# The low half of a folded weight in an attention and feed-forward kernel: subtracted on VectorE before, on TensorE after

## The chip, the cores and the metric

The kernel runs on one core of one Trainium2 chip. The metric is the device time of one execution in microseconds (us), as the median of several runs.

## The reference, cut to what matters

Attention with a local window of 96 keys and 8 global keys (4 batches, 8 heads, 768 positions, 64 numbers a head) gives 3072 tokens of 512 numbers each. On these goes a feed-forward part without a nonlinear function but with a product of two branches:

```
a = x @ w1                    # x: 3072 x 512, w1 and w2: 512 x 1024
b = x @ w2
h = a * b @ w3                # w3: 1024 x 1024
return h @ w_out              # w_out: 1024 x 512
```

Since nothing stands between w3 and w_out, the kernel multiplies these two once, at the start (the fold), and uses the 1024 x 512 product in place of both.

## The kernel before, in words

All of the large products run on TensorE in a rounded format (fp32r, one pass). To keep the accuracy of fp32, each operand is split in a high part (the value rounded to fp32r) and a low part (value minus high part), and three products are summed: high by high, high by low, low by high. This holds for w1 and w2 (tiles `w12h`, `w12l`), for the attention's output (`xh`, `xl`), for a*b (`gh`, `gl`) and for the folded weight (`wh`, and `wl`, eight blocks of 128 x 512).

The fold itself runs in fp32: for each of the eight blocks f, eight products `F.f.k` (L190) are summed over k in one PSUM bank (`prod[f]`, w_ in the rows). Each of these 64 products appears as two matmuls in the trace. Ahead of that VectorE makes the weights from 64-bit input words, three instructions (L168, L170, L172) a piece. When a block is whole, three steps follow, in the order of the names in `ORDER`: `pe.f` (ScalarE copies the bank to SBUF, tile `raw`, L195), `ph.f` (ScalarE rounds `raw` to `wh`, L198), `pl.f` (VectorE subtracts, `wl` = `raw` - `wh`, L203).

The first part of the program is written out by hand as a long string of names, `ORDER`, and runs in that order on every engine. Other names in it are: `S.s`, the scores of step s (TensorE, L577, from `qr` into the tiles `sc` and `more`); `R`, `E`, `s`, `c`, `X`, the softmax of a step (row maxima on VectorE; exponentials L593 on ScalarE; reciprocal of the sums on VectorE; scaling L608 on ScalarE; transposition L619 on VectorE, into `pt`); `V.d`, the values of two steps (TensorE, L633, from `pt` into `sc`); `h.d` and `l.d`, the split of their result (`xh` L656 on ScalarE, `xl` L661 on VectorE); `wh.f` and `wl.f`, the split of a block of w1 and w2 (L179 on ScalarE, L183 on VectorE); `U.f.n.i`, the first feed-forward products (L223 to L225), and `a`, `g`, `gh`, `gl`, the steps behind them; `Z`, the second feed-forward products (L251 to L253). The fold's banks, `more` and the banks of U and Z come from one pool of four PSUM banks, `ps_m`, and a bank is given out again when its last reader is done.

Behind `ORDER` come the other batches in a loop, with the same products and without any fold.

Of the kernel before, what the change touches and what calls it, by code (L numbers as in the profile page):

```python
# [10 lines left out]
F32 = mybir.dt.float32  # L11
F32R = mybir.dt.float32r
BF16 = mybir.dt.bfloat16
I32 = mybir.dt.int32
AF = mybir.ActivationFunctionType
ALU = mybir.AluOpType
PSUM = bass.MemoryType.PSUM

B, H, S, D = 4, 8, 768, 64
DM, DF, DO = 512, 1024, 512  # L20
P = 128
# [6 lines left out]
NFC = DF // P  # L28
WIN = 96
GLB = 8  # L30
R = 32
# [18 lines left out]
FIRST = 5  # L50
# [1 line left out]
nt bias d.h0 d.o0 d.h1 d.o1 A.h0 B.h0 C.h0 d.k1 A.o0 B.o0 d.o2 A.h1 C.o0 F.0.0 d.k2 B.h1 F.1.0 A.o1 d.k3 C.h1 B.o1 F.2.0 A.k1 d.o3 C.o1 F.3.0 B.k1  # L52
A.o2 d.K2 C.k1 A.k2 F.0.1 B.o2 B.k2 F.1.1 C.o2 F.2.1 C.k2 bD biasA d.O2 F.3.1 A.k3 A.o3 B.k3 F.0.2 B.o3 F.1.2 C.k3 d.q0 A.K2 F.2.2 C.o3 F.3.2 d.K3
B.K2 F.0.3 A.O2 F.1.3 C.K2 F.2.3 d.O3 B.O2 S.0 C.O2 F.3.3 d.q1 R.0.0 F.0.4 R.0.1 E.0.0 R.0.2 F.0.5 E.0.1 R.0.3 d.T5 E.0.2 A.K3 F.1.4 E.0.3 B.K3 F.1.5
F.2.4 A.O3 d.W0 B.O3 F.2.5 F.3.4 s.0 C.O3 c.0 F.3.5 S.1 C.K3 d.T4 A.T5 F.0.6 B.T5 F.0.7 d.v0 X.0 F.1.6 pe.0 ph.0 F.2.6 d.T6 R.1.0 R.1.1 E.1.0 F.1.7
C.T5 E.1.1 F.2.7 R.1.2 pe.1 F.3.6 d.q2 R.1.3 E.1.2 F.3.7 pl.0 E.1.3 A.T4 F.5.0 d.T7 pe.3 A.W0 F.5.1 ph.3 s.1 B.T4 c.1 F.5.2 B.W0 F.5.3 d.q3 F.5.4 A.T6
ph.1 F.5.5 X.1 pe.2 ph.2 F.5.6 pl.1 V.0 B.T6 pl.2 C.T6 F.5.7 h.0 C.W0 d.W4 F.6.0 pe.5 l.0 ph.5 F.6.1 wh.0 pl.5 S.2 S.3 d.W3 wl.0 F.6.2 pl.3 R.2.0
F.6.3 R.2.1 E.2.0 F.6.4 R.2.2 E.2.1 R.2.3 F.6.5 C.T4 E.2.2 F.6.6 E.2.3 A.T7 d.W1 s.2 B.T7 c.2 F.6.7 C.T7 d.q5 F.4.0 pe.6 F.4.1 X.2 ph.6 d.v1 F.7.0
R.3.0 F.7.1 R.3.1 E.3.0 R.3.2 F.7.2 d.q4 E.3.1 R.3.3 F.7.3 A.W1 E.3.2 F.7.4 B.W1 E.3.3 F.7.5 s.3 pl.6 F.7.6 c.3 C.W1 F.4.2 F.4.3 wh.1 F.4.4 X.3 F.4.5
wl.1 V.1 A.W3 B.W3 C.W3 F.7.7 h.1 d.W2 F.4.6 wh.3 l.1 F.4.7 pe.7 wl.3 ph.7 S.4 S.5 pe.4 pl.7 ph.4 U.0.0.0 R.4.0 R.4.1 E.4.0 pl.4 U.0.0.1 E.4.1 A.W2  # L60
B.W2 U.0.1.0 a.0 C.W2 U.0.1.1 R.4.2 wh.2 d.W6 R.4.3 U.1.0.0 E.4.2 wl.2 E.4.3 U.1.0.1 g.0 s.4 gh.0 U.1.1.0 A.W4 c.4 gl.0 B.W4 U.1.1.1 C.W4 U.2.0.0 a.1
X.4 wh.4 d.W5 U.2.0.1 g.1 U.2.1.0 a.2 wl.4 gh.1 U.2.1.1 gl.1 A.W6 B.W6 U.3.0.0 C.W6 U.3.0.1 A.W5 wh.6 d.W7 U.3.1.0 B.W5 a.3 U.3.1.1 wl.6 d.v2 C.W5
U.4.0.0 g.2 wh.5 U.4.0.1 g.3 gh.2 wl.5 U.4.1.0 gh.3 a.4 gl.2 U.4.1.1 gl.3 A.W7 B.W7 C.W7 U.5.0.0 d.q7 g.4 wh.7 R.5.0 U.5.0.1 gh.4 R.5.1 d.q6 R.5.2
# [17 lines left out]
class FeedForward:  # L81
# [3 lines left out]
    def __init__(self, ctx, tc, w12, w3k, w3t, w_out, out):  # L85
        self.nc = tc.nc
        self.w12, self.w3k, self.w3t, self.w_out, self.out = w12, w3k, w3t, w_out, out
        self.wp = wp = ctx.enter_context(tc.tile_pool(name="wp", bufs=1))
        self.mp = ctx.enter_context(tc.tile_pool(name="mp", bufs=2))
        self.ps = ctx.enter_context(tc.tile_pool(name="ps_m", bufs=4, space=PSUM))  # L90
        self.w = [wp.tile([P, NFC, 2, NCC, P], F32R, name=f"w12{x}") for x in "hl"]
        self.wh, self.wl = wp.tile([P, NFC, DO], F32R, name="wh"), [None] * NFC
        self.places, self.free, self.raw = list(range(NFC)), [NFC], {}

        self.wo = self.mp.tile([P, NFC, DO], I32, tag="gh", bufs=1, name="wo")
        gl = self.mp.tile([P, 2, 4 * PC], I32, tag="gl", bufs=1, name="stage")
        self.slots = [gl[:, i] for i in range(2)]
        self.t3, self.kt, self.prod, self.got = {}, {}, {}, {}
# [90 lines left out]
        block = self.kt[k // 2][:, (k % 2 * NFH + f) * P:][:, :P] if f < NFH else self.t3[f][:, k * P:(k + 1) * P]  # L189
        self.nc.tensor.matmul(self.prod[f], lhsT=block.bitcast(F32), rhs=self.wo[:, k].bitcast(F32), start=k == 0, stop=k == NFC - 1)  # L190

    def fold_out(self, f):
        i = self.places.pop(0)
        self.raw[f] = i, self.wp.tile([P, DO], F32, tag=f"wl{i}", name=f"raw_{f}")
        self.nc.scalar.activation(self.raw[f][1], self.prod[f], AF.Copy)  # L195

    def fold_high(self, f):
        self.nc.scalar.activation(self.wh[:, f], self.raw[f][1], AF.Copy)  # L198

    def fold_low(self, f):  # L200
        i, raw = self.raw[f]
        self.wl[f] = self.wp.tile([P, DO], F32R, tag=f"wl{self.free.pop()}", name=f"wl_{f}")
        self.nc.vector.tensor_tensor(out=self.wl[f], in0=raw, in1=self.wh[:, f].bitcast(F32), op=ALU.subtract)  # L203
        self.free.append(i)


class Unit:
# [227 lines left out]
def strided(ap, *dims):  # L435

    return bass.AP(ap.tensor, ap.offset, [ap.ap[0], *dims])
# [15 lines left out]
def banded(ctx, tc, ff, ns, nt, n1, nf, oki, qk, vx, sc, pr):  # L453


    nc = tc.nc

    xp = ctx.enter_context(tc.tile_pool(name="xp", bufs=2))
    bp = ctx.enter_context(tc.tile_pool(name="bp", bufs=1))
# [10 lines left out]
    def warm(i):  # L470

        if not warmth:
            x = at.tile([P, P], BF16, tag="pt", name="warm")
            nc.vector.memset(x, 0.0)
            warmth.extend((x, ff.ps.tile([P, 96], F32, tag="m", name="warmed")))
        x, y = warmth
        for _ in range(WARM[i]):
            nc.tensor.matmul(y, lhsT=x[:, :P], rhs=x[:, :96], start=True, stop=True)
# [3 lines left out]
    def distances():  # L482

        n = KF + NR * GLB
        it = bp.tile([P, n], I32, name="it")
        gi = bp.tile([P, NR * GLB], I32, name="gi")
        sl = bp.tile([P, 2], F32, name="sl")
        dist, out = (bp.tile([P, n], F32, name=x) for x in ("dist", "out"))
        gd = bp.tile([P, NR * GLB], F32, name="gd")
        win, glob, own = slice(0, P), slice(P, KF), slice(KF, n)  # L490
        for hp in range(NP):
            x = it[hp * R:(hp + 1) * R]
            nc.gpsimd.iota(x[:, win], pattern=[[-1, P]], base=WIN, channel_multiplier=1)
            nc.gpsimd.iota(x[:, glob], pattern=[[1, GLB]], base=0, channel_multiplier=1)
            nc.gpsimd.iota(x[:, own].rearrange("p (q g) -> p q g", g=GLB), pattern=[[R, NR], [-1, GLB]], base=0, channel_multiplier=1)
        nc.gpsimd.iota(gi.rearrange("p (q g) -> p q g", g=GLB), pattern=[[0, NR], [1, GLB]], base=0, channel_multiplier=0)
        for h in range(H):
            hp, u = divmod(h, 2)
            nc.gpsimd.memset(sl[hp * R:(hp + 1) * R, u:u + 1], -SLOPES[h] / SCALE)
        nc.vector.tensor_copy(out=n1, in_=nt)  # L500
        nb = ff.ps.tile([P, 4], F32, tag="m", name="nb")
        nc.tensor.matmul(nb, lhsT=one, rhs=n1, start=True, stop=True)
        warm(1)
        nc.vector.tensor_copy(out=dist, in_=it)
        nc.vector.tensor_scalar(out=out, in0=dist, scalar1=0.0, scalar2=None, op0=ALU.is_lt)
        nc.scalar.activation(nf, nb, AF.Copy)
        nc.gpsimd.tensor_scalar(out=gd, in0=gi, scalar1=ng, scalar2=FAR, op0=ALU.is_ge, op1=ALU.mult)
        nc.gpsimd.tensor_scalar(out=gd, in0=gd, scalar1=nl, scalar2=None, op0=ALU.max)
        flat = pr.rearrange("p q u w -> p (q u w)").rearrange("p (n k) -> p n k", k=PW * 2 // 3)
        nc.scalar.activation(flat, strided(warmth[0], [0, NR * 3], [1, PW * 2 // 3]), AF.Copy)  # L510
        late.extend((sl, dist, out, gd, own))
# [38 lines left out]
    def frame(s, q):  # L550

        return (0 if s % NB else WIN - R * q), KF
# [48 lines left out]
    def scale(s, engine):  # L601
        sm = stats[s][1]
        if engine is nc.scalar:
            for q in range(NR):
                w0, w1 = frame(s, q)
                for u in range(2):
                    x = pr[:, q, u, GLB + w0:GLB + w1]
                    nc.scalar.activation(x, x, AF.Copy, scale=sm[:, q, u:u + 1])  # L608
        else:
            x = pr[:, :, :, GLB:GLB + KF]  # L610
            nc.vector.tensor_tensor(out=x, in0=x, in1=strided(sm, [2, NR], [1, 2], [0, KF]), op=ALU.mult)
# [64 lines left out]
        warm(0)  # L676

    units = {}
    do = dict(A=lambda *x: ff.convert(0, *x), B=lambda *x: ff.convert(1, *x), C=lambda *x: ff.convert(2, *x), wh=ff.high, wl=ff.low, F=ff.fold, pe=ff.fold_out, ph=ff.fold_high, pl=ff.fold_low, S=scores, R=maxima, E=exponentials, s=sums, c=lambda s: scale(s, nc.scalar if s < FIRST else nc.vector), X=turn, V=values, h=high, l=low, bias=distances, bD=masks, biasA=biases, nt=sizes)
    do.update((name, lambda *x, method=method: getattr(units[0], method)(*x)) for name, method in (("U", "first"), ("a", "gate"), ("g", "product"), ("gh", "high"), ("gl", "low"), ("Z", "second"), ("ot", "store")))  # L680

    def ordered():
# [88 lines left out]
```

## Time and profile before

| | |
|---|---|
| median of 3 runs | 524.25 us (523.61 to 524.45) |
| the profiled execution, its own time | 523.78 us |
| its span, first to last instruction | 521.9 us |
| granted TensorE clock, mean | 1.000 |
| TensorE matmul busy | 514.7 us, 99% of the span |
| TensorE weight loads busy | 404.0 us, 77% |
| VectorE busy | 263.7 us, 51% |
| ScalarE busy | 197.0 us, 38% |

The busy time of TensorE's matmuls counts overlapped instructions once; how fast it advances is read from the distance of the matmuls' starts. About two microseconds of the time lie outside the span. In the rows PE is TensorE, PEld its weight loads, DVE VectorE, ACT ScalarE, POOL GpSimd.

### The profile page before, as it was taken

The page shows a single profiled execution, that of the slowest core. Times are in us where ns is not written, and L with a number is a line of the kernel's source. Part 1 is how long each engine was busy: PE and PEld are TensorE (multiplying, and loading weights), DVE is VectorE, ACT ScalarE, POOL GpSimd, SP SyncE. Part 2 cuts the span into 40 slices and gives each one's busy share as a digit, 9 for nine tenths or more (in the row PEclk, how much of TensorE's full clock was granted, in tenths as well). Part 3 has the DMA queues.
Part 4 walks back from the last instruction along what each step waited for, and adds up shares of the span by engine and source line. Part 5 has one row for each costly group of instructions (what it writes and reads, how often), then busy time and mean ns, then how long its engine had stood idle before and what let it go on. Part 6 is the DMA issues. An engine that isn't in the chain of part 4 may idle for free. (4 is left out here: it accounts for less than half of the span.)

```text
span 521.9 us, 12884 instructions
## 1 busy us (share of the span) xinstructions
PE 514.7 (99%) x5572; PEld 404.0 (77%) x5572; DVE 263.7 (51%) x690; ACT 197.0 (38%) x600; POOL 4.3 (1%) x29
## 2 busy tenths in 40 slices
PE   8999999999999999999999999999999999999997
PEld 5345468888888888888888888888888888888885
DVE  7999999993627337028345046263155352022210
ACT  2557766453435244134243134243253351212210
POOL 2000000000000000000000000000000000000000
PEclk9999999999999999999999999999999999999999
DMA  8997833612350130240130240130240101100001
GB/s 311 370 394 275 344 104 103 267 40 82 120 184 36 36 124 3 63 180 1 62 116 20 76 147 0 48 115 30 93 135 0 64 1 41 43 0 0 1 26 60
DMA packets 13842, 53.71 MB, mean 103 GB/s; under 512 B 1363, under 2 KB 3411, under 8 KB 11731
## 3 DMA queue, kind: packets, MB, share of 16 engines
q1 hardware_dynamic: 13632, 52.57, 27.8%
q8 instruction: 45, 0.74, 0.6%
q10 hardware_dynamic: 146, 0.26, 0.1%
q14 instruction: 19, 0.15, 0.1%
HBM read 46.53 MB, written 6.29 MB: 101 GB/s over the span
## 5 line engine op out<-in xcount | busy, mean ns | idle before, releaser
L223 PE MATMUL m<-xh,w12h 128*128 128x512 f32 x384 | 150.9, 393 | 0.0
L224 PE MATMUL m<-xl,w12h 128*128 128x512 f32 x384 | 149.5, 389 | 0.0
L225 PE MATMUL m<-xh,w12l 128*128 128x512 f32 x384 | 149.4, 389 | 0.0
L223 PEld LDWEIGHTS m<-xh,w12h 128*128 128x128 f32 x384 | 72.1, 188 | 16.7 <-ACT pr L593 1.7
L593 ACT ACTIVATE pr<-pr,mx 128x136 f32<-128x136 f32 (+2 forms) x192 | 74.5, 390 | 26.4 <-DVE mx L586 26.1
L225 PEld LDWEIGHTS m<-xh,w12l 128*128 128x128 f32 x384 | 72.1, 188 | 15.1
L224 PEld LDWEIGHTS m<-xl,w12h 128*128 128x128 f32 x384 | 72.1, 188 | 14.4
L251 PE MATMUL o<-wh,gh 128*128 128x512 f32 x184 | 72.5, 394 | 0.0
L252 PE MATMUL o<-wl,gh 128*128 128x512 f32 x184 | 71.8, 390 | 0.0
L253 PE MATMUL o<-wh,gl 128*128 128x512 f32 x184 | 71.6, 389 | 0.0
L233 DVE TENSOR_TENSOR ag<-m,ag 128x512 f32<-128x512 f32 x48 | 32.8, 685 | 71.5 <-PE m L225 65.8
L238 ACT ACTIVATE gh<-ag 128x512 fp32r<-128x512 f32 x48 | 30.1, 629 | 95.6 <-DVE ag L233 95.6
L661 DVE TENSOR_TENSOR xl<-sc,xh 128x1024 fp32r<-128x1024 f32 x12 | 14.7, 1224 | 73.9 <-ACT xh L656 73.9
L230 ACT ACTIVATE ag<-m 128x512 f32<-128x512 f32 x48 | 28.4, 592 | 46.4 <-PE m L225 44.1
L265 ACT ACTIVATE ot<-o 128x512 f32<-128x512 f32 x23 | 13.8, 599 | 77.7 <-PE o L253 77.7
L243 DVE TENSOR_TENSOR gl<-ag,gh 128x512 fp32r<-128x512 f32 x48 | 32.7, 682 | 16.4 <-ACT gh L238 16.3
L253 PEld LDWEIGHTS o<-wh,gl 128*128 128x128 f32 x184 | 34.5, 188 | 7.6
L251 PEld LDWEIGHTS o<-wh,gh 128*128 128x128 f32 x184 | 34.5, 188 | 7.5 <-issue 0.2
L252 PEld LDWEIGHTS o<-wl,gh 128*128 128x128 f32 x184 | 34.5, 188 | 6.9
L619 DVE STREAM_TRANSPOSE pt<-pr 128x1280 f32<-128x1280 f32 x24 | 36.1, 1506 | 1.3 <-ACT pr L608 1.2
L593 ACT ACTIVATION_READ_ACCUMULATOR pr<-pr,mx 128x1 f32 x192 | 36.1, 188 | 0.0
L633 PEld LDWEIGHTS sc<-pt,vr 32*64 32x64 f32 x2112 | 30.5, 130 | 5.0 <-issue 4.3
(97 smaller groups left out, 421.0 us busy)
## 6 DMA issues: line engine op xcount, KB each, us to landing
qr<-qk SPq DMA_DIRECT2D x20, 720.0 KB, 6.4
vr<-vx SPq DMA_DIRECT2D x8, 768.0 KB, 4.4
out_dram<-ot SPq DMA_DIRECT2D x23, 256.0 KB, 2.0
raws<-w SPq DMA_DIRECT2D x5, 1024.0 KB, 4.9
stage<-w3t SPq DMA_DIRECT2D x3, 1024.0 KB, 7.7
vr<-vx SPq DMA_DIRECT2D x4, 576.0 KB, 3.8
qr<-qk SPq DMA_DIRECT2D x4, 528.0 KB, 7.5
more_raws<-w SPq DMA_DIRECT2D x2, 1024.0 KB
```

The source lines that it names most:

```text
L223: self.nc.tensor.matmul(ps, lhsT=mh, rhs=xh[:, i], start=i == 0, stop=False)
L224: self.nc.tensor.matmul(ps, lhsT=mh, rhs=xl[:, i], start=False, stop=False)
L225: self.nc.tensor.matmul(ps, lhsT=ml, rhs=xh[:, i], start=False, stop=i == NCC - 1)
L233: self.nc.vector.tensor_tensor(out=self.g[f], in0=self.ps[f, 1], in1=self.a[f], op=ALU.mult)
L238: self.nc.scalar.activation(self.gh[:, f], self.g[f], AF.Copy)
L243: self.nc.vector.tensor_tensor(out=self.gl[:, f], in0=self.g[f], in1=self.gh[:, f].bitcast(F32), op=ALU.subtract)
L251: self.nc.tensor.matmul(ps, lhsT=self.gh[:, f, ts], rhs=ff.wh[:, f], start=f == 0, stop=False)
L252: self.nc.tensor.matmul(ps, lhsT=self.gh[:, f, ts], rhs=ff.wl[f], start=False, stop=False)
L253: self.nc.tensor.matmul(ps, lhsT=self.gl[:, f, ts], rhs=ff.wh[:, f], start=False, stop=f == NFC - 1)
L593: nc.scalar.activation(x, x, AF.Exp, bias=mx[:, q, u:u + 1], scale=-1.0, accum_out=sm[:, q, u:u + 1])
L619: nc.vector.transpose(strided(pts[d][:, half * 2 * NR * PF:], [PF, 2 * NR], [P, NR + 1], [1, R]), x.rearrange("p n (k c) -> p n k c", c=R))
L633: nc.tensor.matmul(sc[cols, hp, n0 * R:n1 * R], lhsT=v[rows, i, cols], rhs=turned, start=i == i0, stop=i == NV - 1, skip_group_check=True)
```

## The change

The same two halves of a folded block are made in another way. ScalarE rounds the bank straight to `wh` (`pe.f` is now `fold_high`). TensorE then multiplies `wh` by minus the unit matrix and adds the result onto the same bank, so that the bank holds value minus high part (`ph.f` is now `fold_rest`). ScalarE copies the bank to `wl` (`pl.f` is now `fold_low`). The tiles `raw` go, VectorE's eight subtractions go, and the bank of a block is given back after the second copy instead of the first. Minus the unit matrix is made once, at the start, by two GpSimd instructions and one ScalarE copy. In `ORDER` the names `ph` and `pl` stand at other places.

```diff
-F.2.4 A.O3 d.W0 B.O3 F.2.5 F.3.4 s.0 C.O3 c.0 F.3.5 S.1 C.K3 d.T4 A.T5 F.0.6 B.T5 F.0.7 d.v0 X.0 F.1.6 pe.0 ph.0 F.2.6 d.T6 R.1.0 R.1.1 E.1.0 F.1.7
+F.2.4 A.O3 d.W0 B.O3 F.2.5 F.3.4 s.0 C.O3 c.0 F.3.5 S.1 C.K3 d.T4 A.T5 F.0.6 B.T5 F.0.7 d.v0 X.0 F.1.6 pe.0 F.2.6 d.T6 R.1.0 R.1.1 E.1.0 F.1.7 ph.0
...
-        self.places, self.free, self.raw = list(range(NFC)), [NFC], {}
+        self.minus = wp.tile([P, P], F32R, name="minus")
...
-    def fold_out(self, f):
-        i = self.places.pop(0)
-        self.raw[f] = i, self.wp.tile([P, DO], F32, tag=f"wl{i}", name=f"raw_{f}")
-        self.nc.scalar.activation(self.raw[f][1], self.prod[f], AF.Copy)
-
     def fold_high(self, f):
-        self.nc.scalar.activation(self.wh[:, f], self.raw[f][1], AF.Copy)
+        self.nc.scalar.activation(self.wh[:, f], self.prod[f], AF.Copy)
+
+    def fold_rest(self, f):
+
+        self.nc.tensor.matmul(self.prod[f], lhsT=self.minus, rhs=self.wh[:, f], start=False, stop=True, skip_group_check=True)
 
     def fold_low(self, f):
-        i, raw = self.raw[f]
-        self.wl[f] = self.wp.tile([P, DO], F32R, tag=f"wl{self.free.pop()}", name=f"wl_{f}")
-        self.nc.vector.tensor_tensor(out=self.wl[f], in0=raw, in1=self.wh[:, f].bitcast(F32), op=ALU.subtract)
-        self.free.append(i)
+        self.wl[f] = self.wp.tile([P, DO], F32R, tag=f"wl{f}", name=f"wl_{f}")
+        self.nc.scalar.activation(self.wl[f], self.prod[f], AF.Copy)
...
+        eye = bp.tile([P, P], F32, name="eye")
+        make_identity(nc, eye)
...
+        nc.scalar.activation(ff.minus, eye, AF.Copy, scale=-1.0)
```

The order of the instructions on each engine, read at three places. First TensorE and ScalarE around blocks 0 and 1, ahead of the values of the first two steps (`V.0`). A block's bank is a w_ with a number of its own: block 0 is w_221 before and w_228 after, block 1 is w_225 and w_232, block 3 is w_236 and w_243, block 5 is w_457 and w_465. TensorE before:

```order
L577 MATMUL sc<-qr_331 32x136 x32
L190 MATMUL w_221<-wo,kt_352 128x512 x2
L190 MATMUL w_225<-wo,kt_352 128x512
L190 MATMUL w_231<-wo,kt_352 128x512
L190 MATMUL w_225<-wo,kt_352 128x512
L190 MATMUL w_231<-wo,kt_352 128x512
L190 MATMUL w_236<-wo,kt_352 128x512 x2
L190 MATMUL w_457<-wo,t_5_411 128x512 x7
L633 MATMUL sc<-pt_418,vr_416 64x128 x8
```

and TensorE of the change:

```order
L577 MATMUL sc<-qr_338 32x136 x32
L190 MATMUL w_228<-wo,kt_359 128x512 x2
L190 MATMUL w_232<-wo,kt_359 128x512
L190 MATMUL w_238<-wo,kt_359 128x512
L190 MATMUL w_232<-wo,kt_359 128x512
L197 MATMUL w_228<-wh,minus 128x512
L190 MATMUL w_238<-wo,kt_359 128x512
L190 MATMUL w_243<-wo,kt_359 128x512 x2
L197 MATMUL w_232<-wh,minus 128x512
L190 MATMUL w_465<-wo,t_5_418 128x512 x3
L197 MATMUL w_243<-wh,minus 128x512
L190 MATMUL w_465<-wo,t_5_418 128x512 x4
```

Three new products (L197) stand between fold products; the fold products keep their order. ScalarE before, from block 0's copy on:

```order
L195 ACTIVATE raw_421<-w_221 128x512
L198 ACTIVATE wh<-raw_421 128x512
L593 ACTIVATE pr,sm_427<-pr,mx_426 128x136 x4
L195 ACTIVATE raw_441<-w_225 128x512
L593 ACTIVATE pr,sm_427<-pr,mx_426 128x136 x4
L195 ACTIVATE raw_460<-w_236 128x512
L198 ACTIVATE wh<-raw_460 128x512
L608 ACTIVATE pr<-pr,sm_427 128x136 x8
L198 ACTIVATE wh<-raw_441 128x512
```

and ScalarE of the change:

```order
L193 ACTIVATE wh<-w_228 128x512
L593 ACTIVATE pr,sm_432<-pr,mx_431 128x136 x2
L201 ACTIVATE wl_441<-w_228 128x512
L593 ACTIVATE pr,sm_432<-pr,mx_431 128x136 x2
L193 ACTIVATE wh<-w_232 128x512
L593 ACTIVATE pr,sm_432<-pr,mx_431 128x136 x2
L201 ACTIVATE wl_459<-w_232 128x512
L593 ACTIVATE pr,sm_432<-pr,mx_431 128x136 x2
L193 ACTIVATE wh<-w_243 128x512
L608 ACTIVATE pr<-pr,sm_432 128x136 x8
```

Five copies stand ahead of the scaling (L608) before and after, but two of them, the `wl`, now read a bank that TensorE must first have written again. Second place: TensorE at the scores of steps 2 and 3 (block 6 is w_575 before and w_580 after, block 7 w_707 and w_710, block 4 w_697 and w_699). Before:

```order
L577 MATMUL sc<-qr_444 32x136 x16
L577 MATMUL sc<-qr_479 32x136 x32
L190 MATMUL w_575<-wo,t_6_482 128x512 x6
L190 MATMUL w_697<-wo,t_4_455 128x512 x2
L190 MATMUL w_707<-wo,t_7_679 128x512 x7
```

and in the change:

```order
L577 MATMUL sc<-qr_451 32x136 x16
L197 MATMUL w_465<-wh,minus 128x512
L577 MATMUL sc<-qr_488 32x136 x32
L190 MATMUL w_580<-wo,t_6_491 128x512 x6
L190 MATMUL w_699<-wo,t_4_463 128x512 x2
L197 MATMUL w_580<-wh,minus 128x512
L190 MATMUL w_710<-wo,t_7_681 128x512 x7
```

One new product stands between two runs of small matmuls, and one between fold products of other blocks. Third place: the end of the fold, blocks 7 and 4, ahead of the first product of `U`. ScalarE before:

```order
L179 ACTIVATE w12h<-t3s 128x1024
L195 ACTIVATE raw_863<-w_707 128x512
L198 ACTIVATE wh<-raw_863 128x512
L195 ACTIVATE raw_933<-w_697 128x512
L198 ACTIVATE wh<-raw_933 128x512
L593 ACTIVATE pr,sm_946<-pr,mx_945 128x136 x4
```

and ScalarE of the change:

```order
L179 ACTIVATE w12h<-t3s 128x1024
L193 ACTIVATE wh<-w_710 128x512
L201 ACTIVATE wl_933<-w_710 128x512
L193 ACTIVATE wh<-w_699 128x512
L201 ACTIVATE wl_937<-w_699 128x512
L593 ACTIVATE pr,sm_947<-pr,mx_946 128x136 x4
```

TensorE there before:

```order
L577 MATMUL sc<-qr_721 32x136 x16
L577 MATMUL sc<-qr_695 32x136 x32
L223 MATMUL m_0_0_938<-xh_570,w12h 128x512
L224 MATMUL m_0_0_938<-xl_571,w12h 128x512
L225 MATMUL m_0_0_938<-xh_570,w12l 128x512
```

and of the change:

```order
L577 MATMUL sc<-qr_724 32x136 x16
L577 MATMUL sc<-qr_697 32x136 x32
L197 MATMUL w_710<-wh,minus 128x512
L197 MATMUL w_699<-wh,minus 128x512
L220 MATMUL m_0_0_939<-xh_575,w12h 128x512
L221 MATMUL m_0_0_939<-xl_576,w12h 128x512
```

The `wh` of block 4 stands behind the `wl` of block 7 on ScalarE, and the two new products stand next to each other on TensorE. On VectorE nothing changes but that the eight L203 are gone; on the DMA queues nothing changes.

## Rows read from the trace of the kernel before

**Rows 1.** The page's busy times: us, share of the span, instructions.

```profile
PE 514.7 (99%) x5572; PEld 404.0 (77%) x5572; DVE 263.7 (51%) x690; ACT 197.0 (38%) x600; POOL 4.3 (1%) x29
```

**Rows 2.** TensorE's waits over the whole span: total us, times, longest.

```profile
PE w L190 <- DVE wo L172: 1.2, 3, 0.8
PE warmed L478 <- DVE warm L474: 1.1, 1, 1.1
PE w L190 <- DVE kt L172: 1.0, 1, 1.0
```

**Rows 3.** One stage: length, then busy us of PE, PEld, DVE, ACT, POOL.

```profile
33.00:124.00 91.00, 91.00 (x1076) 62.22 (x1057) 82.49 (x167) 54.05 (x154) 0.00 (x0) 1.00 0.50 188
```

**Rows 4.** TensorE in order of time, 25 to 79 us: start, length, count.

```profile
25.01 7.13 PE L190 MATMUL w<-wo,kt 128*128 128x512 f32 x16 [0.78 <-DVE wo L172]
...
33.20 7.13 PE L190 MATMUL w<-wo,kt 128*128 128x512 f32 x16
40.17 6.17 PE L190 MATMUL w<-wo,t 128*128 128x512 f32 x14
46.27 2.33 PE L633 MATMUL sc<-pt,vr 32*64 32x128 f32 x144
48.53 2.84 PE L190 MATMUL w<-wo,t 128*128 128x512 f32 x6
51.30 0.69 PE L577 MATMUL more<-qr 64*32 64x136 f32 x32
51.79 1.66 PE L577 MATMUL sc<-qr 64*32 64x136 f32 x96
...
77.49 0.50 PE L223 MATMUL m<-xh,w12h 128*128 128x512 f32 x1
77.82 0.39 PE L224 MATMUL m<-xl,w12h 128*128 128x512 f32 x1
```

**Rows 5.** TensorE in order of time: two matmuls of U, 105 starts apart.

```profile
80.12 0.39 PE L225 MATMUL m<-xh,w12l 128*128 128x512 f32 x1
...
103.92 0.39 PE L225 MATMUL m<-xh,w12l 128*128 128x512 f32 x1
```

**Rows 6.** TensorE in order of time where the kind of matmul changes.

```profile
77.28 0.28 PE L577 MATMUL sc<-qr 64*32 64x136 f32 x1
...
301.34 0.39 PE L253 MATMUL o<-wh,gl 128*128 128x512 f32 x1
301.66 0.69 PE L577 MATMUL more<-qr 64*32 64x136 f32 x32
```

**Rows 7.** Groups by line and shape, 0 to 180 us: busy us, mean ns.

```profile
L593 ACT ACTIVATE pr<-pr,mx 128x136 f32<-128x136 f32 x68 | 26.8, 395 | 7.4 <-DVE mx L586 7.4
L203 DVE TENSOR_TENSOR wl<-raw,wh 128x512 fp32r<-128x512 f32 x8 | 5.4, 679 | 0.0
```

**Rows 8.** ScalarE in order of time: start, length, and idle before with its releaser.

```profile
15.47 0.72 ACT L525 ACTIVATE biasw<-dist,sl 128x512 bf16<-128x512 f32 x1 [10.30 <-DVE dist L517]
...
35.22 0.60 ACT L195 ACTIVATE raw<-w 128x512 f32<-128x512 f32 x1 [2.58 <-PE w L190]
...
41.53 2.49 ACT L608 ACTIVATE pr<-pr,sm 128x136 f32<-128x136 f32 x8
...
48.64 1.03 ACT L656 ACTIVATE xh<-sc 128x1024 fp32r<-128x1024 f32 x1 [2.96 <-PE sc L633]
...
76.02 0.64 ACT L198 ACTIVATE wh<-raw 128x512 fp32r<-128x512 f32 x1
76.56 0.58 ACT L195 ACTIVATE raw<-w 128x512 f32<-128x512 f32 x1
...
80.54 0.60 ACT L230 ACTIVATE ag<-m 128x512 f32<-128x512 f32 x1 [1.17 <-PE m L225]
```

**Rows 9.** VectorE in order of time, two of its instructions.

```profile
44.18 1.51 DVE L619 STREAM_TRANSPOSE pt<-pr 128x1280 f32<-128x1280 f32 x1
...
50.18 1.22 DVE L661 TENSOR_TENSOR xl<-sc,xh 128x1024 fp32r<-128x1024 f32 x1
```

More of the change, by code (lines that the diff above doesn't have):

```diff
@@ L54 @@
 B.K2 F.0.3 A.O2 F.1.3 C.K2 F.2.3 d.O3 B.O2 S.0 C.O2 F.3.3 d.q1 R.0.0 F.0.4 R.0.1 E.0.0 R.0.2 F.0.5 E.0.1 R.0.3 d.T5 E.0.2 A.K3 F.1.4 E.0.3 B.K3 F.1.5
-F.2.4 A.O3 d.W0 B.O3 F.2.5 F.3.4 s.0 C.O3 c.0 F.3.5 S.1 C.K3 d.T4 A.T5 F.0.6 B.T5 F.0.7 d.v0 X.0 F.1.6 pe.0 ph.0 F.2.6 d.T6 R.1.0 R.1.1 E.1.0 F.1.7
[L56 to L60, printed above, removed]
+F.2.4 A.O3 d.W0 B.O3 F.2.5 F.3.4 s.0 C.O3 c.0 F.3.5 S.1 C.K3 d.T4 A.T5 F.0.6 B.T5 F.0.7 d.v0 X.0 F.1.6 pe.0 F.2.6 d.T6 R.1.0 R.1.1 E.1.0 F.1.7 ph.0
+pl.0 C.T5 E.1.1 F.2.7 R.1.2 pe.1 F.3.6 d.q2 R.1.3 E.1.2 F.3.7 ph.1 pl.1 E.1.3 A.T4 F.5.0 d.T7 pe.3 A.W0 F.5.1 s.1 B.T4 c.1 F.5.2 ph.3 pl.3 B.W0 F.5.3
+d.q3 F.5.4 A.T6 F.5.5 X.1 pe.2 F.5.6 V.0 ph.2 pl.2 B.T6 C.T6 F.5.7 h.0 C.W0 d.W4 F.6.0 pe.5 l.0 F.6.1 wh.0 S.2 ph.5 pl.5 S.3 d.W3 wl.0 F.6.2 R.2.0
+F.6.3 R.2.1 E.2.0 F.6.4 R.2.2 E.2.1 R.2.3 F.6.5 C.T4 E.2.2 F.6.6 E.2.3 A.T7 d.W1 s.2 B.T7 c.2 F.6.7 C.T7 d.q5 F.4.0 pe.6 F.4.1 X.2 d.v1 ph.6 pl.6
+F.7.0 R.3.0 F.7.1 R.3.1 E.3.0 R.3.2 F.7.2 d.q4 E.3.1 R.3.3 F.7.3 A.W1 E.3.2 F.7.4 B.W1 E.3.3 F.7.5 s.3 F.7.6 c.3 C.W1 F.4.2 F.4.3 wh.1 F.4.4 X.3 F.4.5
+wl.1 V.1 A.W3 B.W3 C.W3 F.7.7 h.1 d.W2 F.4.6 wh.3 l.1 F.4.7 pe.7 wl.3 S.4 S.5 ph.7 pl.7 pe.4 ph.4 pl.4 U.0.0.0 R.4.0 R.4.1 E.4.0 U.0.0.1 E.4.1 A.W2
 B.W2 U.0.1.0 a.0 C.W2 U.0.1.1 R.4.2 wh.2 d.W6 R.4.3 U.1.0.0 E.4.2 wl.2 E.4.3 U.1.0.1 g.0 s.4 gh.0 U.1.1.0 A.W4 c.4 gl.0 B.W4 U.1.1.1 C.W4 U.2.0.0 a.1
@@ L678, in banded @@
     units = {}
-    do = dict(A=lambda *x: ff.convert(0, *x), B=lambda *x: ff.convert(1, *x), C=lambda *x: ff.convert(2, *x), wh=ff.high, wl=ff.low, F=ff.fold, pe=ff.fold_out, ph=ff.fold_high, pl=ff.fold_low, S=scores, R=maxima, E=exponentials, s=sums, c=lambda s: scale(s, nc.scalar if s < FIRST else nc.vector), X=turn, V=values, h=high, l=low, bias=distances, bD=masks, biasA=biases, nt=sizes)
+    do = dict(A=lambda *x: ff.convert(0, *x), B=lambda *x: ff.convert(1, *x), C=lambda *x: ff.convert(2, *x), wh=ff.high, wl=ff.low, F=ff.fold, pe=ff.fold_high, ph=ff.fold_rest, pl=ff.fold_low, S=scores, R=maxima, E=exponentials, s=sums, c=lambda s: scale(s, nc.scalar if s < FIRST else nc.vector), X=turn, V=values, h=high, l=low, bias=distances, bD=masks, biasA=biases, nt=sizes)
     do.update((name, lambda *x, method=method: getattr(units[0], method)(*x)) for name, method in (("U", "first"), ("a", "gate"), ("g", "product"), ("gh", "high"), ("gl", "low"), ("Z", "second"), ("ot", "store")))
```

## The prediction

> **What bounds the kernel now.** I read the page's busy times first. TensorE's matmuls are busy for 99% of the span, VectorE for 51% and ScalarE for 38% [rows 1]. That is an average, and the change touches one stage, so the second view is that stage: from 33 to 124 us VectorE is busy for 82.49 of 91.00 us and TensorE's matmuls for all 91.00, at a granted clock of 1.00 [rows 3]. Two engines look full there, and only one can set the pace. Busy time of overlapping matmuls cannot tell which, so I read two more views.
>
> The first is the list of TensorE's waits. Over the whole span it holds three groups, 1.2, 1.1 and 1.0 us [rows 2], and in order of time the last of these waits ends at 25.01 us [rows 4], ahead of the first copy of a finished block at 35.22 us [rows 8]. The second is the distance of starts. Sixteen matmuls of the fold take from 33.20 to 40.17 us; without 0.10 us for a restart (the first gap of U is 0.33 where the next ones are 0.23) that is 0.43 us each [rows 4]. From 40.17 to 46.27 us it is fourteen in 6.10 us, again 0.43 each and 0.09 for the change to the small matmuls [rows 4]. In U 105 starts take 23.80 us, 0.227 us each [rows 5]. From 33 us on TensorE goes from one matmul to the next at a constant distance, with a fixed extra where the kind of matmul changes. It waits for nobody. The time is TensorE's queue from 33 us to the end, and whatever is added to that queue is added to the time.
>
> **What the change removes.** Eight subtractions on VectorE, 679 ns each, 5.4 us in all [rows 7]. TensorE waits for VectorE nowhere after 25 us [rows 2], so this shortens nothing; it only gives VectorE slack. I take 0. The bounds are 0 and, if every one had been on the path, minus 8 x 0.60 (the 0.68 overlap the next instruction a little), 4.8 us; that is a rival below.
>
> **What it adds at the start.** Two GpSimd instructions and one ScalarE copy of 128 x 128. ScalarE is idle for 10.30 us up to 15.47 us, waiting for VectorE's distances [rows 8], and the copy lies in that gap. The GpSimd pair is not in this trace; it would cost something only if it held up `gd` for those 10 us. 0.
>
> **What ScalarE does.** Two copies a block before, two after; sizes and sources differ little (0.58 to 0.64 us a copy [rows 8]; I take 0.60 for the new ones, nearest to these). What is new is not its length but its place in line: a `wl` copy waits until TensorE has run the new product, and everything behind it on ScalarE waits too.
>
> **What TensorE gets.** Eight products of 128 x 128 by 128 x 512 in fp32r. The nearest row is U, same shape and format: 0.227 us each [rows 5]. It isn't lower than that, since 105 starts in a row show no shorter pace. By the Trainium skill, page "TensorE: Matmul & The Clock Gate", section "Back-to-back issue gap", a stream of weight loads and matmuls of 512 columns comes at about 131 ns each; eight would then be an estimated 1.0 us rather than 1.8 and my sum 0.8 lower, but this case's own stream says 227.
>
> *Blocks 0, 1, 3 and 6* stand between fold products. Both kinds fill the whole array with 512 columns, so I take no extra for the change of format: 4 x 0.23 = 0.92. No row shows fp32 beside fp32r without small matmuls between; the upper bound is the change to small matmuls and back, 0.09 + 0.10 more for each, 0.76 for four. *Block 2* follows V.0, where a switch was paid already: 0.23.
>
> *Block 5* stands between the scores of steps 2 and 3, which ran on without a break. It brings two switches: small to large 0.21 (77.28 to 77.49 [rows 4, 6]) and large to small 0.32 (301.34 to 301.66 [rows 6]), against about 0.02 between two of the 96 small ones: 0.51.
>
> *Blocks 7 and 4* are the costly place. TensorE meets the product of block 7 after the scores, and the product of block 4 right behind it. The latter needs `wh` of block 4, and on ScalarE that copy stands behind `wl` of block 7, which needs the product of block 7. So the two engines hand over to and fro with nothing else in TensorE's queue. From the start of product 7: 0.39 until its end, 0.03 to wake ScalarE (80.12 + 0.39 to 80.54 [rows 5, 8]), 0.54 until the next copy can start (76.02 to 76.56 [rows 8]), 0.60 for `wh` of block 4, and 0.03 to wake TensorE (taken as the other way round): 1.59. Then product 4 runs, 0.33 to the first product of U as after a standstill, and 0.23 on. Before it was scores, 0.21, U, 0.33, U. So 1.59 + 0.33 + 0.23 - 0.33 = 1.82 more. Queued behind the waiting product is all of U; VectorE and ScalarE wait for it too.
>
> **Waits that could be new, and their margins.** Product 1 needs `wh` of block 1. TensorE gets to product 0 after five folds from 33.20: 33.20 + 0.10 + 5 x 0.86 = 37.60, ends it at 37.99, and is at product 1 at 37.60 + 0.23 + 3 x 0.86 = 40.41. ScalarE: `wl` of block 0 from 38.02, the next copy or exponential 0.54 later, a pair of exponentials 0.79 [rows 7], `wh` 0.60: 39.95. Margin 0.46. Product 3: `wl` of block 1 from 40.83, 0.54, a pair 0.79, `wh` 0.60 = 42.76, against TensorE at 40.41 + 0.23 + 2.58 = 43.22. Margin 0.46. The scaling behind it starts at 42.76 instead of 41.53 [rows 8], so the transposition at 44.18 [rows 9] comes 1.2 later and ends at about 46.9; V.0 starts at 46.27 + 3 x 0.23 = 46.96 [rows 4] and reads it after 16 of its 144 matmuls (2.26 us), at 47.2. Margin 0.3. After V.0, `wl` of block 2 stands ahead of `xh` on ScalarE: product 2 from 48.53 + 0.69 = 49.22 [rows 4] to 49.61, `xh` (48.64 before [rows 8]) from 50.18 to 51.21, `xl` (50.18 before [rows 9]) to 52.43; the scores that overwrite `sc` come at 51.79 + 0.92 = 52.71 [rows 4]. Margin 0.28. All hold, by little. I take 0, and up to 0.3 for each of the four as an upper bound, 1.2.
>
> **The sum.** 0.92 + 0.23 + 0.51 + 1.82 = 3.48 us, of which 1.8 is plain work and the rest standstill and switching. On the profiled execution's 523.78 us (span 521.9) that gives 527.3. This execution lies 0.47 below the median of its runs, so for the median I say **527.6** (+0.64%).
>
> **The rivals.**
> - *VectorE sets the pace* up to 124 us, so taking 4.8 us off it pays, and the products vanish in TensorE's idle time: 524.25 - 4.8 = 519.5, or 523 if the products count. For it speaks 82.49 of 91.00 us [rows 3]; against it that TensorE, which would have to wait for VectorE, doesn't after 25 us [rows 2]. It would decide if the starts in 33 to 124 us showed gaps; they show none [rows 4, 5]. The Trainium skill, page "Perfetto Trace Analysis", section "Identifying the Most-Contended Engine", says that matmul busy time doesn't tell how full TensorE is, and to use weight-load busy time beside the others' occupancy. In this stage that is 62.22 of 91.00 us, 68%, against VectorE's 91% [rows 3], and by that rule VectorE would be the full engine; the starts speak against it. 3 in 100.
> - *No standstill at blocks 7 and 4*: the product of block 4 finds its `wh` ready, and switches cost less. Then 8 x 0.23 and 0.3: 526.3. The order of ScalarE speaks against it. 12 in 100.
> - *The thin margins fail or each format switch is paid*: 0.76 and 0.3 to 1.2 on top, 528.7 to 529.6. For it: four margins under 0.5 us, made from sums of five or six rows. 18 in 100.
> - *Lost in the rest*: something elsewhere gives back 2.5 us or more, within 0.2% of before, 524.3 to 525.2. Nothing in the rows does. 5 in 100.
> - The forecast, 526.9 to 528.4: 62 in 100.
>
> **How the numbers follow.** A difference of 0.2%, 1.05 us, is about what this measurement tells from none. The range leaves out the first and fourth rival (8) and the far end of the third: 526.0 to 529.2. Faster 0.03, same 0.05, slower 0.92.
>
> **What would show it.** Eight L197 on TensorE; those of blocks 0, 1, 3 and 6 with 0.23 us to the next start. One wait of TensorE for ScalarE of about 1.2 us near 80 us, between the seventh and the eighth, at an unchanged clock. VectorE's busy time down by 5.4 us, with more idle. The first product of U 3.5 us later, and the same 3.5 at the end. It would be wrong if the starts before 79 us moved by much more than 1.7, which would mean one of the four margins, or if TensorE's queue lost gaps that the rows above don't show.

## The result, and the profile after

The changed kernel takes 527.98 us (median of 3 runs, 527.83 to 528.23) against 524.25 us before: a ratio of 1.0077, 95% interval 1.0064 to 1.0091. That is 3.7 us slower, 0.4 us above the predicted 527.6 and inside the range.

The page's busy times of the changed kernel stand against [rows 1]:

```profile
span 526.2 us, 12897 instructions
PE 517.1 (98%) x5580; PEld 405.1 (77%) x5580; DVE 259.3 (49%) x682; ACT 196.2 (37%) x601; POOL 4.9 (1%) x31
```

VectorE lost eight instructions and 4.4 us. They were 5.4 us as a sum of rows [rows 7], but each overlapped the one behind it, so one was worth 0.55 us of VectorE's time. TensorE has eight instructions more. The span grew by 4.3 us in this pair of profiled executions. TensorE's waits over the whole span, as in [rows 2] (total us, times, longest):

```profile
PE w L190 <- DVE wo L172: 1.6, 3, 0.9
PE w L197 <- ACT wh L193: 1.2, 1, 1.2
...
```

One wait is of the new kind: 1.2 us, once, in a product (L197) for ScalarE's rounded block (L193). The others lie ahead of the stage. TensorE in order of time through the stage with the eight products, which answers to [rows 4] (start, length, engine, line, operation, count, idle before with its releaser):

```profile
33.83 4.56 PE L190 MATMUL w<-wo,kt 128*128 128x512 f32 x10
37.83 0.80 PE L197 MATMUL w<-wh,minus 128*128 128x512 f32 x1
38.46 2.74 PE L190 MATMUL w<-wo,kt 128*128 128x512 f32 x6
40.63 0.80 PE L197 MATMUL w<-wh,minus 128*128 128x512 f32 x1
...
47.60 2.33 PE L633 MATMUL sc<-pt,vr 32*64 32x128 f32 x144
...
52.87 0.69 PE L577 MATMUL more<-qr 64*32 64x136 f32 x32
...
54.02 0.50 PE L197 MATMUL w<-wh,minus 128*128 128x512 f32 x1
54.45 1.20 PE L577 MATMUL sc<-qr 64*32 64x136 f32 x64
55.58 7.13 PE L190 MATMUL w<-wo,t 128*128 128x512 f32 x16
...
78.32 1.66 PE L577 MATMUL sc<-qr 64*32 64x136 f32 x96
79.91 0.49 PE L197 MATMUL w<-wh,minus 128*128 128x512 f32 x1
81.58 0.50 PE L197 MATMUL w<-wh,minus 128*128 128x512 f32 x1 [1.18 <-ACT wh L193]
81.92 0.39 PE L220 MATMUL m<-xh,w12h 128*128 128x512 f32 x1
82.15 0.39 PE L221 MATMUL m<-xl,w12h 128*128 128x512 f32 x1
```

The products are there (those of blocks 3, 2 and 6 are left out; 3 and 6 look like the first two), and the wait is between the last two. Don't read the length of the first ones: the row of a product behind a fold starts 0.03 us after the start of the fold half ahead of it and lasts 0.80. What it costs is read from the starts. Ten fold halves begin at 33.83 (the first has 0.10 for a restart), so the tenth is at 33.83 + 0.10 + 9 x 0.43 = 37.80; the next fold half is at 38.46, 0.66 later instead of 0.43. That is 0.23 for the product.

**The stage as a measure.** From here on I count from the start of the fold at F.0.6 to the second product of U: 33.20 to 77.82 = 44.62 us before [rows 4], 33.83 to 82.15 = 48.32 us after, 3.70 us more. Behind it nothing changes: 521.9 - 77.82 = 444.1 before, 526.2 - 82.15 = 444.1 after. Ahead of it the profiled execution after lost 0.63 us more (33.83 against 33.20), where TensorE waits for the first loads and their conversion. This part wanders from execution to execution, as the experiments show, and nothing found ties it to the change.

Why 1.2 us of wait: ScalarE in order of time, against [rows 8], the last three rows (the first two belong to the copy of the unit matrix at the start, to which I come back at the end).

```profile
3.85 0.30 ACT L508 ACTIVATE minus<-eye 128x128 fp32r<-128x128 f32 x1
...
15.73 0.72 ACT L525 ACTIVATE biasw<-dist,sl 128x512 bf16<-128x512 f32 x1 [10.37 <-DVE dist L517]
...
77.03 0.59 ACT L193 ACTIVATE wh<-w 128x512 fp32r<-128x512 f32 x1
80.44 0.60 ACT L201 ACTIVATE wl<-w 128x512 fp32r<-128x512 f32 x1 [2.82 <-PE w L197]
80.93 0.59 ACT L193 ACTIVATE wh<-w 128x512 fp32r<-128x512 f32 x1
```

ScalarE stands idle for 2.82 us; the copy for block 4 (80.93) is queued behind one that needs the product of block 7 (80.44). The product starts at 79.91, ScalarE starts at 80.44, the next copy at 80.93, it ends at 81.52, and the product of block 4 starts at 81.58.

### The profile page after: what moved, and what is told of

Its sections match the earlier page's. It is cut to its first block, busy times and chain, and to the rows that moved or that the text cites. A ratio compares the mean times of both kernels' runs of the same rounds, so it can differ in the third digit from the quotient of the medians.

```text
span 526.2 us, 12897 instructions
## 1 busy us (share of the span) xinstructions
PE 517.1 (98%) x5580; PEld 405.1 (77%) x5580; DVE 259.3 (49%) x682; ACT 196.2 (37%) x601; POOL 4.9 (1%) x31
```

## The theories

- **A, the prediction's**: TensorE's queue sets the time of this stage. The price is eight products at 0.23, block 5's place between two scores, and the standstill at blocks 7 and 4. VectorE's relief is worth nothing.
- **B**: VectorE sets the pace up to 124 us; the relief pays and something else costs more.
- **C**, formed for the 0.63 us ahead of the stage: the unit matrix and its negative, made at the start, hold up the first loads or their conversion.

All ratios below are against the kernel before, with 95% intervals; the kernel before had medians of 524.0, 524.04 and 523.58 us in the three groups of runs, and each ratio goes by the median of its own group. The one profiled execution of each kernel gives its stage.

## The experiments

**The rounding of block 4 ahead of the low part of block 7.** One item of the order is moved, so that ScalarE rounds block 4 before it waits for the product of block 7. The pieces of the order's line:

```diff
-S.4 S.5 ph.7 pl.7 pe.4 ph.4 pl.4 U.0.0.0
+S.4 S.5 pe.4 ph.7 ph.4 pl.7 pl.4 U.0.0.0
```

> The change with one thing reordered: on ScalarE the rounded half of block 4 is made before the low half of block 7 instead of after it; TensorE's order is the same. Theory A (TensorE's queue sets the time, and the standstill between the products of blocks 7 and 4, 1.67 us from start to start, is a hand-over with ScalarE): both products find their operand ready, the step shrinks to about 0.23, so 1.4 us less than the change, about 526.5 us, 2.2 above before. Theory B (VectorE sets the pace in this stage, so TensorE's standstill is hidden): no difference to the change, 528.0. Theory C (the loss sits at the start, where the unit matrix is made): no difference, 528.0.

Measured: 526.16 us, ratio 1.0037 (1.0024 to 1.0049). TensorE in order of time at that place:

```profile
79.89 0.73 PE L197 MATMUL w<-wh,minus 128*128 128x512 f32 x2
...
80.68 0.40 PE L221 MATMUL m<-xl,w12h 128*128 128x512 f32 x1
```

and ScalarE's rounding of block 4, ahead of the products:

```profile
77.91 0.60 ACT L193 ACTIVATE wh<-w 128x512 fp32r<-128x512 f32 x1 [0.31 <-PE w L190]
```

Both products now run as a pair and the wait is gone. The stage is 80.68 - 33.81 = 46.87 us, 1.45 less than with the change: the standstill's whole price, with all eight products still in the queue.

**Block 5's product behind both scores.**

```diff
-wh.0 S.2 ph.5 pl.5 S.3 d.W3 wl.0
+wh.0 S.2 S.3 ph.5 pl.5 d.W3 wl.0
```

> The change with the product of block 5 moved from between the scores of steps 2 and 3 to behind both, ahead of a fold product. Theory A: inside the scores it costs two switches of matmul kind, 0.64 us; behind them it costs about 0.23, as block 2's behind the values does. So 0.4 us less than the change, about 527.6. A rival within A: it only moves the switch, and nothing is gained, 528.0. Theories B and C: 528.0.

Measured: 527.92 us, ratio 1.0077 (1.0065 to 1.0089); no gain. The stage is 81.39 - 32.71 = 48.68 us, 0.36 more than with the change. TensorE in order of time:

```profile
51.74 0.69 PE L577 MATMUL more<-qr 64*32 64x136 f32 x32
...
53.82 0.50 PE L197 MATMUL w<-wh,minus 128*128 128x512 f32 x1
54.16 7.03 PE L190 MATMUL w<-wo,t 128*128 128x512 f32 x16
61.68 0.50 PE L197 MATMUL w<-wh,minus 128*128 128x512 f32 x1 [0.49 <-ACT wh L193]
62.02 9.60 PE L190 MATMUL w<-wo,t 128*128 128x512 f32 x22
```

and ScalarE:

```profile
54.36 0.60 ACT L201 ACTIVATE wl<-w 128x512 fp32r<-128x512 f32 x1 [2.14 <-PE w L197]
...
61.05 0.58 ACT L193 ACTIVATE wh<-w 128x512 fp32r<-128x512 f32 x1
```

where the change has:

```profile
54.56 0.60 ACT L201 ACTIVATE wl<-w 128x512 fp32r<-128x512 f32 x1 [1.21 <-PE w L197]
```

The place itself gave what was expected, to 0.02 us: from the start of the scores to the next fold half it is 54.16 - 51.74 = 2.42 us instead of 55.58 - 52.87 = 2.71, and the fold behind it has no restart of 0.10 left to pay, 0.39 won in all. But ScalarE's `wl` copy now comes 2.62 us after the scores began (51.74 to 54.36) instead of 1.69 (52.87 to 54.56). The exponentials and the scaling stand behind it, and behind those the rounding of block 6, which ends at 61.63. TensorE had begun the last of sixteen fold halves at 54.16 + 15 x 0.43 = 60.61, so the product could have run at 61.04; it starts at 61.68, 0.64 late, and the next start comes 0.34 behind it (62.02) instead of 0.23. Together that is 0.75 us lost for 0.39 won, which is the 0.36 by which the stage is longer. My expectation followed the moved item and not what stood behind it on ScalarE.

**Both moves together.**

> The change with both reorderings: ScalarE rounds block 4 ahead of the low half of block 7, and the product of block 5 stands behind the scores of steps 2 and 3. Theory A: what is left is eight products at 0.23 us, 1.8 above before, about 526.1; no order of the same steps gets below that, since the queue holds the eight products. Theory B: 528.0 or any value that follows VectorE.

Measured: 526.62 us, ratio 1.0045 (1.0032 to 1.0059), where the first move alone had 1.0037. The stage is 80.11 - 32.90 = 47.21 us, as the two parts make it (48.32 - 1.45 + 0.36 = 47.23). The wait at block 6 is there again, and the one at block 4 gone; TensorE's wait for ScalarE in this run's list:

```profile
PE w L197 <- ACT wh L193: 0.5, 1, 0.5
```

**Both moves, and the low part of block 5 emptied late.** On top of both moves, the `wl` copy of block 5 goes behind the exponentials of step 2, still ahead of the scaling of the scores:

```diff
-wh.0 S.2 S.3 ph.5 pl.5 d.W3 wl.0 F.6.2 R.2.0
+wh.0 S.2 S.3 ph.5 d.W3 wl.0 F.6.2 R.2.0
...
-F.6.6 E.2.3 A.T7
+F.6.6 E.2.3 pl.5 A.T7
```

> The run with both reorderings, and the low half of block 5 taken out of ScalarE's way: it stands behind the exponentials of step 2 and ahead of the scaling, where ScalarE waits half a microsecond for VectorE, instead of ahead of the exponentials. Theory A, refined by the last runs (moving block 5's product saved its switches, but its low half then came 0.9 us later on ScalarE, and through exponentials and scaling the rounded half of block 6 came late for TensorE): the wait at block 6 goes, and what is left is eight products at 0.23: about 525.9, 1.9 above before, 0.5 to 0.8 below the run with both reorderings. The rival within A: the wait at block 6 stays near 1 us, because it is the scores and not the low half that hold up the exponentials: 526.6.

Measured: 526.27 us, ratio 1.0044 (1.0027 to 1.0061). TensorE in order of time:

```profile
54.16 7.03 PE L190 MATMUL w<-wo,t 128*128 128x512 f32 x16
60.63 0.79 PE L197 MATMUL w<-wh,minus 128*128 128x512 f32 x1
61.26 9.60 PE L190 MATMUL w<-wo,t 128*128 128x512 f32 x22
...
78.39 0.73 PE L197 MATMUL w<-wh,minus 128*128 128x512 f32 x2
...
79.19 0.40 PE L221 MATMUL m<-xl,w12h 128*128 128x512 f32 x1
```

and ScalarE:

```profile
56.89 0.57 ACT L201 ACTIVATE wl<-w 128x512 fp32r<-128x512 f32 x1
...
59.92 0.57 ACT L193 ACTIVATE wh<-w 128x512 fp32r<-128x512 f32 x1
```

No product waits for ScalarE any more: the fold starts at 54.16 as in the run with block 5's product moved alone, and the fold half behind block 6's product comes at 61.26 instead of 62.02. So it was the `wl` copy that held up the exponentials, and the rival within A falls. The stage begins at 32.72 and is 79.19 - 32.72 = 46.47 us, 1.85 more than before: 8 x 0.23 and nothing else. With eight products in a queue that shows no gap I take this as the floor for the stage; no run shows that no other order gets below it. It is still slower than before. The whole-kernel times of these three don't separate them (1.0037, 1.0045 and 1.0044 with overlapping intervals); the order 46.87, 47.21, 46.47 rests on the stages of one execution each. In the last kernel the expected gain of 0.5 to 0.8 us over the run with both moves does not show in the median at all (2.69 us above its group's kernel before, where that run had 2.58): four of its six executions took 526.2 to 526.6 us, and the profiled one is one of the other two, at 524.76.

**No product at all.** The method with the product is left empty; ScalarE then copies the whole block as its low part, so the second part of w3 times w_out is the whole block instead of its rest.

```diff
-        self.nc.tensor.matmul(self.prod[f], lhsT=self.minus, rhs=self.wh[:, f], start=False, stop=True, skip_group_check=True)
+        pass
```

> The change without its eight products (the low half is then a copy of the whole block, so what is summed later is not the reference's); everything else stays, VectorE's eight subtractions stay away, the unit matrix is made and unused. Theory A: TensorE's queue is that of before again, so 524.3 us, 3.7 below the change, although VectorE has 5.4 us less to do than before. Theory B: the relief of VectorE shows at last, 519.5 to 521. Theory C: about 525, since the late start of the fold stays and only part of the difference goes.

Measured: 524.09 us, ratio 0.9998 (0.9987 to 1.0008). The stage's windows against [rows 3] (length, then busy us of PE, PEld, DVE, ACT, POOL, granted clock, share of DMA, GB/s):

```profile
33.00:124.00 91.00, 91.00 (x1082) 62.24 (x1068) 78.25 (x159) 52.88 (x155) 0.00 (x0) 1.00 0.50 187
```

TensorE in order of time:

```profile
33.60 7.13 PE L190 MATMUL w<-wo,kt 128*128 128x512 f32 x16
...
46.67 2.34 PE L633 MATMUL sc<-pt,vr 32*64 32x128 f32 x144
48.94 2.84 PE L190 MATMUL w<-wo,t 128*128 128x512 f32 x6
51.71 0.69 PE L577 MATMUL more<-qr 64*32 64x136 f32 x32
...
53.79 16.57 PE L190 MATMUL w<-wo,t 128*128 128x512 f32 x38
...
78.23 0.40 PE L221 MATMUL m<-xl,w12h 128*128 128x512 f32 x1
```

This decides between A and B. VectorE is relieved by 4.2 us in the stage (82.49 to 78.25) and ScalarE doesn't wait for products; the stage is 78.23 - 33.60 = 44.63 us, that of before to 0.01. Taking work off VectorE moves nothing, and B falls. The run bears on C too: it makes the unit matrix, and its median is 0.1 us above before, at most 0.4 by the interval, where C wanted about 525.

**Each product twice.** The second product takes another rounded block off, so the low part is off by one rounded block.

```diff
-        self.nc.tensor.matmul(self.prod[f], lhsT=self.minus, rhs=self.wh[:, f], start=False, stop=True, skip_group_check=True)
+        for _ in range(2):
+            self.nc.tensor.matmul(self.prod[f], lhsT=self.minus, rhs=self.wh[:, f], start=False, stop=True, skip_group_check=True)
```

> The change with each of the eight products issued twice in a row (the low half is then off by a further rounded block, so the sum is not the reference's). Theory A with 0.23 us a product and no price for the switch between fp32 and fp32r: 8 x 0.227 = 1.8 more than the change, about 529.8, TensorE's eight second products 0.23 behind the first ones or paid for by the next fold product. If the first product of each pair pays a switch that the second doesn't, the same 1.8; if every product drains the bank before the next may write it, 0.4 to 0.6 each, 531 to 533. Theory B: 528.0, hidden.

Measured: 530.27 us, ratio 1.0118 (1.0102 to 1.0134). TensorE in order of time:

```profile
34.05 4.56 PE L190 MATMUL w<-wo,kt 128*128 128x512 f32 x10
38.05 1.03 PE L198 MATMUL w<-wh,minus 128*128 128x512 f32 x2
...
83.42 0.74 PE L198 MATMUL w<-wh,minus 128*128 128x512 f32 x2 [1.18 <-ACT wh L193]
...
84.23 0.39 PE L222 MATMUL m<-xl,w12h 128*128 128x512 f32 x1
```

The stage is 84.23 - 34.05 = 50.18 us, 1.86 more than with the change, 0.23 for each added product wherever it stands: a second product into the same bank needs no more than its place. The wait at block 4 is 1.18 as in the changed kernel. The median is 6.27 us above before, 0.7 more than the stage makes; in the profiled execution TensorE has one wait of 0.6 us behind the stage for which the profile names no engine, and I leave the rest open.

**VectorE subtracts again, from the bank.** The change's order stays, the product goes, and VectorE forms the low part from the bank and the rounded block (one subtraction, the separate copy of the block stays away). In the second kernel the unit matrix and its negative go too; in the first they are made and not used.

```diff
-        self.nc.scalar.activation(self.wl[f], self.prod[f], AF.Copy)
+        self.nc.vector.tensor_tensor(out=self.wl[f], in0=self.prod[f], in1=self.wh[:, f].bitcast(F32), op=ALU.subtract)
```

> The change with the subtraction done by VectorE straight from the bank (no product on TensorE, one copy less on ScalarE a block, the unit matrix made and unused, the order of names that of the change). Theory A: TensorE's queue is that of before, VectorE's and ScalarE's work is off the path: 524.3, within 0.3 of before, unless a bank that is held longer stops a fold product. Theory B: VectorE has its eight subtractions again, so as before, 524.3, but together with the run without products this tells: B wants that run 4 to 5 us below this one, A wants them equal. Theory C: 525.

> As the run with VectorE subtracting from the bank, but the unit matrix isn't made at all. Theories A and B: equal to that run within 0.2 us, 524.3. Theory C (the GpSimd pair and ScalarE's copy hold up the start by 0.6 us): 0.6 less than that run.

Measured: 524.6 us, ratio 1.0007 (0.9998 to 1.0016), with the unit matrix; 524.25 us, ratio 1.0000 (0.9991 to 1.0009), without. The first kernel's TensorE around V.0:

```profile
46.87 2.56 PE L633 MATMUL sc<-pt,vr 32*64 32x128 f32 x144
49.36 2.90 PE L190 MATMUL w<-wo,t 128*128 128x512 f32 x6
```

and the second's:

```profile
33.63 7.13 PE L189 MATMUL w<-wo,kt 128*128 128x512 f32 x16
...
46.70 0.47 PE L629 MATMUL sc<-pt,vr 32*64 32x128 f32 x16
47.53 2.12 PE L629 MATMUL sc<-pt,vr 32*64 32x160 f32 x128 [0.36 <-DVE pt L615]
49.58 2.90 PE L189 MATMUL w<-wo,t 128*128 128x512 f32 x6
```

with VectorE's transposition there:

```profile
45.98 1.50 DVE L615 STREAM_TRANSPOSE pt<-pr 128x1280 f32<-128x1280 f32 x1
```

The first came out 0.56 us above its group's kernel before, where I had said at most 0.3, and 0.35 above the second, where A wanted 0.2 at most and C 0.6. The scatter of the executions is as large, so this pair decides nothing about C. C falls by the run without products. What the stages add (78.71 - 33.80 = 44.91 and 78.94 - 33.63 = 45.31, 0.29 and 0.69 us more than before) lies mostly at V.0: it takes 49.36 - 46.87 = 2.49 us in the first and 49.58 - 46.70 = 2.88 in the second, against 48.94 - 46.67 = 2.27 without products or subtractions. In the second the wait is in the list: the transposition ends at 47.48, and V.0 goes on at 47.53. In the first the longer V.0 shows no wait of its own, and that it has the same cause is argued. At this one spot VectorE's timing can reach TensorE; it is the third of the prediction's four margins. In the kernel before it did not: the transposition ended at 44.18 + 1.51 = 45.69 [rows 9], ahead of the start of V.0 at 46.27, and V.0 took 48.53 - 46.27 = 2.26 [rows 4].

**The change again**, in the last group of runs.

> The change once more, beside the others on the same chip: 3.6 to 4.0 above before, about 527.8; its first fold product starts anywhere between 7.2 and 8 us, since that depends on when the first loads land.

Measured: 527.6 us, ratio 1.0075 (1.0058 to 1.0093). The stage begins at 32.98 and is 81.29 - 32.98 = 48.31 us, against 48.32 in the first execution, while the start of the stage moved by 0.85 us. Over all these kernels the stage begins between 32.71 and 34.05 us, in no order that follows what was changed (33.20 and 33.63 without the unit matrix, 32.71 to 34.05 with it).

## Why the prediction was right

- **TensorE's queue is the time.** Confirmed: without products the stage is that of before to 0.01 us, and doubled products add 0.23 each. The rival by which VectorE sets the pace falls with the same two runs: 4.2 us off VectorE gave nothing. The rule of the Trainium skill, page "Perfetto Trace Analysis", section "Identifying the Most-Contended Engine", names two measures for TensorE to set beside the others' occupancy, its work as a share of the peak and weight-load busy time. The prediction worked out only the second; by it VectorE would have been named, and the runs go against that.
- **Blocks 0, 1, 3 and 6**: 0.23 each, 0.92 predicted. Measured 0.92: from the stage's start to V.0 it is 47.60 - 33.83 = 13.77 us instead of 46.27 - 33.20 = 13.07, 0.70 for three, and 0.22 at block 6. The change of format between whole-array products costs nothing extra. The Trainium skill, page "TensorE: Matmul & The Clock Gate", section "Back-to-back issue gap", has 131 ns for a pair of weight load and matmul of 512 columns in a stream, without naming a number format; these fp32r products don't agree, since each second product took 0.23.
- **Block 2**: 0.23 predicted, 0.24 measured (52.87 - 47.60 = 5.27 from V.0 to S.2 instead of 5.03).
- **Block 5**: 0.51 predicted, 0.63 measured. From the start of S.2 to the next fold it is 55.58 - 52.87 = 2.71 us, without products 53.79 - 51.71 = 2.08. The product, alone behind small matmuls, needs 0.43 to the next score; I took 0.32 from a row in which it stood behind others of its kind.
- **Blocks 7 and 4**: 1.82 predicted, 1.91 measured (from 78.32 to 82.15 instead of from 75.90 to 77.82). From product to product it is 81.58 - 79.91 = 1.67 us where I had 1.59. The size was off by the wake-up of ScalarE, 0.53 from the product's start where I took 0.42; the copy behind it came sooner, 0.49 instead of 0.54, and TensorE's wake-up was 0.06 instead of 0.03.
- **The sum**: 3.48 predicted, 0.92 + 0.24 + 0.63 + 1.91 = 3.70 measured. The two terms that fell short, by 0.12 and 0.09, both begin with a first product behind small matmuls, which I priced by a product in a row of products. The median I gave has a slip besides: 523.78 + 3.48 + 0.47 is 527.73, not 527.6, so 0.13 of the 0.38 us between forecast and result is arithmetic and not the kernel.
- **The four margins** held in the changed kernel: behind 33 us its list has no wait of TensorE but the one at block 4. So the 0 taken for them was right. The third, at V.0, failed only where VectorE subtracts in the change's order. The product of block 6 was a fifth place of the same kind that the prediction didn't list. In the changed kernel its rounding was ready in time; moving block 5's product used it up.
- **What the change removes**: 0 predicted for the time, and nothing found. VectorE's busy time fell by 4.4 us and not by the 5.4 announced, which was a sum of overlapping rows.
- **The unit matrix at the start**: 0 predicted, and nothing found, though the run without products bounds it only to 0.4 us. ScalarE's copy of it (3.85 us) takes 0.30, and behind it ScalarE is still idle for 10.37 us up to 15.73.

One of the prediction's signs of being wrong needs the stage as its zero: the starts before 79 us moved by 78.32 - 75.90 = 2.42 us, more than the 1.7 it allowed, but 0.63 of it came ahead of the stage and is not the change's.

Why the start of the stage moves by up to 1.34 us between executions I didn't settle beyond this: it begins at different times with and without the unit matrix, and TensorE's waits there are for loads and for VectorE's conversion of what they bring.

No version with the product beats the kernel before; the best, at 1.0037 and 1.0044, still pays 1.85 us of plain work or more. Without it (0.9998, 1.0007 and 1.0000) nothing separates the kernels from the one before.

## What to carry to other kernels

Where one engine's starts follow each other without gaps, as TensorE's did here, added work on it cost its start distance, however short, and relief of another engine that looked almost full was worth nothing; read the gaps and not the shares. A product in that queue which depends on another engine costs the whole hand-over when nothing else stands in the queue, 1.67 us here from product to product: 1.45 of 3.70 us came back by moving one ScalarE copy ahead of the one that waits. And before moving an item in a written-out order, follow what stands behind it on the slower engine to the next point at which the full engine waits: the gain of 0.39 us at block 5 came back as a loss of 0.75 at block 6.

## What the hardware showed

- A 128 x 128 by 128 x 512 product in fp32r between fp32 fold products costs 0.23 us of TensorE's time, the same as in a row of its own kind; there was no price for the change of format.
- The first such product after small matmuls or a standstill takes longer to the next start: 0.34 (81.58 to 81.92), 0.43 back to small ones (54.02 to 54.45). ScalarE, which reads its bank, starts 0.53 us after the product's start (79.91 to 80.44).
- The stage repeated far better than its start: 48.32 and 48.31 us in two executions of the changed kernel, whose stages began 0.85 us apart.
